# Top-k attention and ELU feed-forward on one core: in the first six steps, the mask begins where the selection ends, extra key transposes are spread, and raw weight tiles use other buffers

## The chip, the cores and the metric

One core of a Trainium2 chip runs the whole kernel. The metric is the device time of one execution, in microseconds (us); lower is better. Engines are named as in the profile: PE is TensorE (PEld its weight load), DVE is VectorE, ACT is ScalarE, POOL is GpSimd, SP is SyncE, which issues nearly all DMAs.

## What is computed

Attention over 8 batches, 8 heads, 576 tokens of 64 elements, in which each query keeps its 32 best keys, and then a two-layer network with ELU. The weights come as float64.

```python
scores = scale * np.matmul(q, k.transpose(0, 1, 3, 2))
kth = np.partition(scores, -top_k, axis=-1)[..., -top_k:-top_k + 1]
scores = np.where(scores >= kth, scores, -1000000000.0)
attn = np.exp(scores - np.max(scores, axis=-1, keepdims=True))
attn = attn / (np.sum(attn, axis=-1, keepdims=True) + 1e-09)
attn_out = np.matmul(attn, v)                      # (8, 8, 576, 64)
x = attn_out.transpose(0, 2, 1, 3).reshape(4608, 512)
h = x @ w_in                                       # (512, 2048)
g = np.where(h > 0.0, h, np.exp(np.minimum(h, 0.0)) - 1.0)
out = g @ w_out                                    # (2048, 512)
```

## The kernel before

**Steps.** The work is cut into 144 steps. A step is one tile of 128 query rows of a batch with one pair of heads (a pair of half tiles at the end of a batch). The order on every engine is the order in which the code is written: nothing is rescheduled, and each engine works through its own queue in order, waiting on semaphores where an input is not there. Step n of the loop (L676) holds the selection of tile n ("now"), the softmax and transposes of tile n-1 ("last"), and from step 6 on the attention product of tiles further back. A step does the following.

- `first_max` and `next_max` (L333 to L348), on DVE: eight largest of a row (MAX8, L336 and L348), strike them out (MATCH_REPLACE8, L342), four times over for two heads. This is the selection of the 32 best.
- the mask. From step 6 on `mask` (L357) does it on POOL with three operations for each half. For the tiles of steps 0 to 5 `mask_early` (L364) does it: a small `field` operation on DVE (L374), three small ones on POOL (L377, L378, L381: `minus`, `nth`, `pos`), then for each half an ACT activation (L386) and a POOL subtraction (L389), and at last `neg` (L355), which the exponential needs.
- `exp` (L398) on ACT, `trans` (L438, L456) on PE with copies on ACT (L443, L457): the transposed probabilities. `attend` (L471): the attention product on PE, and after the last pair of heads a copy to `xT` (L481).
- `sums` and `normalise`: the row sums' reciprocals are written to DRAM and read back as a broadcast (`recd`, `rb`, L413 and L425), and POOL multiplies `xT` by them (L486).
- `feed` puts pieces of the feed-forward network between: `hidden` (L506 on PE, L520 to L522 on ACT: `n`, `gT`, `n`; L523 on POOL) and `project` (L530). How many go into a step is worked out from counts alone when the program is built.

**Keys and queries.** `load_qk` loads a pair of heads from DRAM, `transpose_qk` turns it on PE (L268, L276; ten transposes into two PSUM tiles) and copies it to SBUF on ACT (L273, L281), and `keep_kq` stores it in DRAM, from where `load_kq` gets it again for later steps. The first four pairs belong to batch 0. Pairs 4 to 9 ("extra") are turned ahead of their need in steps 3, 4 and 5, and from step 7 on one pair in every second step (`turns`). The transposes, the scores (L311) and the probabilities share a pool of two PSUM tiles, so each of them waits until ACT has copied an earlier one out.

**Weights.** Each of 32 units of weights comes as raw float64 words and is turned into float32 in the first seven steps: `split_weight` on ACT (L185, L186, two activations), and two slots later `join_weight` on DVE (L191, L192) and POOL (the add of L196). `decode` places slots: four in each of steps 0 to 3 (places 3 to 6), six in steps 4 and 5, four in step 6. Slot i joins unit i-2 and splits unit i. So slots 18 to 23 lie in step 4, 24 to 29 in step 5 and 30 to 33 in step 6. Raw words lie in the pool "g", in spare buffers s1 to s4, or in rows of `w_out` that are not yet filled; the list `loads` (L144) says for each load its unit, its count, its home, and the unit that must have been joined first. In an early step the order after the start is:

```python
decode(n, 0); feed(n, 0.5); exp(last, 0); exp(last, 1)
next_max(now, (n, 1)); decode(n, 2); trans(last); feed(n, 0.5)
next_max(now, (n, 3)); decode(n, 4)
...                                   # sums(last), attend(last)
next_max(now, (n, 5)); decode(n, 6)
...                                   # normalise(last.g), extra transposes, loads
```

`mask_early(last)` stands at the very start of a step, ahead of the scores of a later step and after the last decode of the step before.

Of the kernel before, what the change touches and what calls it, by code (L numbers as in the profile page):

```python
# [11 lines left out]
U32 = mybir.dt.uint32  # L12
# [49 lines left out]
def kernel(  # L62
# [60 lines left out]
    WN = 512  # L123
    NW = 2 * NF
    raw = {}
    decoded = [0]

    def spare_tile(i, name):

        size = ((2 * J + 2) * P, 2 * S, 2 * WN)[i // 2]  # L130
        return spare.tile([P, size], FP32, tag=f"s{i}", name=name)
# [9 lines left out]

    loads = [(0, 3, "g", -1), (3, 1, "raw", -1), (4, 3, "g", -1), (7, 1, "raw", -1)]  # L144
    loads += [(8, 4, "w", -1), (12, 4, "w", -1), (16, 3, "g", 2), (25, 1, "raw", -1)]
    loads += [(26, 1, "raw", -1), (27, 1, "raw", 3), (19, 3, "g", 6)]
    loads += [(28, 1, "raw", 7), (22, 3, "w", 15), (29, 1, "raw", 25)]
    loads += [(30, 1, "raw", 26), (31, 1, "raw", 27)]
    places_in_w_out = {8: 0, 12: 8, 22: 10}

    turn = [0]

    def load_weights(most=NW, margin=1):

        while loads and most > 0 and (
            loads[0][3] < 0 or loads[0][3] + margin < decoded[0]
        ):
            i, n, home, _ = loads.pop(0)
            most -= 1
            if home == "w":  # L160
                at = places_in_w_out[i]
                t = w_out[:, at : at + 2 * n, :].bitcast(U32)
                t = t.rearrange("p (c f) d -> p c (f d)", f=2)
            elif home == "g":
                t = gpool.tile([P, n, 2 * WN], U32, tag="g", name="raw")[:]
            else:
                t = spare_tile(1 + turn[0] % 4, "raw")[:, 0 : 2 * WN].bitcast(U32)
                t = t.rearrange("p (c n) -> p c n", c=1)
                turn[0] += 1
            if i < NF:  # L170
                f, c = divmod(i, NC)
                src = moe_w_in[c * P : (c + n) * P, 2 * f * WN : 2 * (f + 1) * WN]
            else:
                src = moe_w_out[(i - NF) * P : (i - NF + n) * P, :]
            nc.sync.dma_start(t, src.rearrange("(c p) n -> p c n", p=P))
            for j in range(n):
                raw[i + j] = t[:, j, :]
# [38 lines left out]
    def load_qk(b, hp):  # L216

        first = b == 0 and hp < 3
        aside = (b, hp) in ((0, 1), (0, 2), (1, 1), (1, 2), (2, 0))
        if aside:  # L220
            home = xtpool.tile([P, 2, NC * T // 2], FP32, tag="xT", name="kqin")
            home = home[:, :, 0 : (J + 1) * 2 * D].rearrange(
                "p n (j h d) -> p n j h d", j=J + 1, h=2
            )
        for n, (name, src) in enumerate((("k", k), ("q", q))):
            queue = nc.scalar if first and name == "q" else nc.sync
            if aside:
                t = home[:, n]
            else:
                t = ldpool.tile([P, J + 1, 2, D], FP32, tag="in", name=name + "in")  # L230
            queue.dma_start(
                t[:, 0:J, :, :],
                src[b, 2 * hp : 2 * hp + 2, 0:JP, :].rearrange(
                    "h (p j) d -> p j h d", j=J
                ),
            )
            queue.dma_start(
                t[0:R, J, :, :],
                src[b, 2 * hp : 2 * hp + 2, JP:S, :].rearrange("h p d -> p h d"),
            )  # L240
            loaded[b, hp, name] = t
# [343 lines left out]
    EARLY = 6  # L585
    sizes = {0: (1, 1, 1, 1, 1, 1, 1, 2), 2: (2, 2, 2, 3), B - 2: (3, 3, 2, 1)}
    steps, first, order = [], {}, []
    for b in range(B):
# [4 lines left out]
        for qt in (0, 1, 2, 3, 4) if b % 2 == 0 else (4, 0, 1, 2, 3):  # L593
            r0 = b * S + (JP if qt == J else qt)
            if qt == J:
# [3 lines left out]
                c0, n = slot * P + (b % 2) * R, R  # L599
                rows = slice(r0, r0 + R)  # L600
            else:
                blk, slot = places.pop(0)
                c0, n = slot * P, P
# [20 lines left out]
    def decode(n, place):  # L624

        if place in ((1, 2, 3, 4, 5, 6) if n in (4, 5) else (3, 4, 5, 6)):
            weight_slot()
# [5 lines left out]

    pairs = [(b, hp) for b in range(B) for hp in range(NHP)]

    extra = {3: (4, 5, 6), 4: (7, 8), 5: (9,)}
    fetch = {2: (4, 5, 6), 3: (7, 8), 4: (9,), 5: (10,)}
    for p, pair in enumerate(pairs):
        if p >= NHP:
            n = next((n for n in extra if p in extra[n]), None)  # L640
            if n is None:
                n = EARLY + 1 + 2 * (p - 10)
                turns[n] = pair
            at(n + 1, keep_kq, *pair)
        elif p >= 2:
            at(p - 1, keep_kq, *pair)
# [11 lines left out]
    with tc.manual_schedule():  # L658
        for hp in range(3):
            load_qk(0, hp)  # L660
        load_weights(3)
        for hp in range(2):
            transpose_qk(0, hp)
            steps[hp].kq = {hp: kqT[0, hp]}
            for half in range(2):
                scores(steps[hp], half)
            if hp == 0:
                load_qk(0, 3)
        load_weights()
        load_v(0, 0)  # L670
        first_max(steps[0])
        weight_slot()
        weight_slot()
        for hp in range(2):
            keep_kq(0, hp)
        for n in range(NS + 4):  # L676
            early = n < EARLY
            now, last, done = (
                steps[n + d] if 0 <= n + d < NS else None for d in (0, -1, -2)
            )  # L680
            for fn, args in todo.pop(n, []):
                fn(*args)
            gone = None
            if early:
                if last:
                    mask_early(last)
                if n + 2 < NHP:
                    transpose_qk(0, n + 2)
                for m in direct.get(n, ()):
                    hp = m % NHP  # L690
                    steps[m].kq = {hp: kqT[0, hp]}
                    for half in range(2):
                        scores(steps[m], half)
            elif n % 2 == 0:

                for d in (2, 3):
                    if n + d < NS:
                        for half in range(2):
                            scores(steps[n + d], half)
                    if d == 2:  # L700
                        for u in steps[n - 4 : n - 2]:
                            if not u.attended:
                                attend(u)
                                gone = u
            if n in turns:
                transpose_qk(*turns[n])
            if n >= EARLY and n + 2 in turns:
                load_qk(*turns[n + 2])
            if now and n > 0:
                first_max(now)  # L710
            if last and not early:
                biases(last, early)
                mask(last, 0)
            if early:
                decode(n, 0)
                feed(n, 0.5)
                if last:
                    exp(last, 0)
                    exp(last, 1)
                next_max(now, (n, 1))  # L720
                decode(n, 2)
                if last:
                    trans(last)
                feed(n, 0.5)
                next_max(now, (n, 3))
                decode(n, 4)
                if last and last.ends:
                    load_weights(margin=0)
                    sums(last)
                if last:  # L730
                    attend(last)
                next_max(now, (n, 5))
                decode(n, 6)
                if last and last.ends:
                    normalise(last.g)
                for p in extra.get(n, []):
                    transpose_qk(*pairs[p])
                for p in fetch.get(n, []):
                    load_qk(*pairs[p])
                continue  # L740
            decode(n, 0)
            feed(n, (0.3, 0.7)[n % 2])
            if now:
                next_max(now, (n, 1))
            decode(n, 2)
            if last:
                mask(last, 1)
                exp(last, 0)
            if done and not done.turned:
                trans(done)  # L750
            if now:
                next_max(now, (n, 3))
            decode(n, 4)
            if gone and gone.ends:
                normalise(gone.g)
            feed(n, (0.3, 0.7)[n % 2])
            if now:
                next_max(now, (n, 5))
            decode(n, 6)
            if last:  # L760
                exp(last, 1)
            if done and done.ends and not done.summed:
                sums(done)
        while ffn:
            ffn.pop(0)[1]()
# [33 lines left out]
```

## Time and profile before

| | |
|---|---|
| time, median of 3 (lowest to highest) | 1663.04 us (1661.5 to 1663.15) |
| the profiled execution | 1664.04 us, of which its span is 1662.3 |
| busy: PE, DVE, POOL, ACT | 1571.1, 1455.5, 1142.7, 925.7 us |
| the chain that ended last, by engine | PE 60%, DVE 24%, POOL 5%, issue 4%, ACT 4% |
| DVE busy in 0 to 20, 20 to 40, 40 to 60 us | 8.06, 17.46, 19.32 |
| mean granted PE clock | 0.974 |

The span runs from the first to the last instruction. Busy time is summed by engine; the chain is followed back from the last instruction, from each to what released it. A list in order of time shows for each instruction its start, its length, its line, its tiles, and in brackets how long the engine was idle ahead of it and what ended that. The table of stretches gives for each stretch the busy time of PE, PEld, DVE, ACT and POOL, the granted PE clock as a share of full speed, and the share and the rate of the transfers. Line numbers are those of the kernel before; behind L144 the changed kernel's are smaller by 3, as its list is shorter.

### The profile page before, as it was taken

How to read it: one execution, taken by the hardware profiler on the slowest of the kernel's cores; microseconds unless marked ns; L12 is line 12 of the kernel's file. 1: busy time of each engine (PE TensorE's matmuls, PEld its weight loads, DVE VectorE, ACT ScalarE, POOL GpSimd, SP SyncE). 2: the span in 40 equal slices, each digit the busy share in tenths (PEclk: the TensorE clock that was granted, in tenths of full speed). 3: DMA queues.
4: the chain of work that ended last, by engine and by line, in shares of the span. 5: the costliest groups of instructions: out<-in, count | busy, mean ns of one | idle time of the engine just before them, and what ended most of it. 6: DMA issues, size and time to landing. Idle time of an engine off the chain costs nothing.

```text
span 1662.3 us, 28290 instructions
## 1 busy us (share of the span) xinstructions
PE 1571.1 (95%) x9792; PEld 1046.9 (63%) x9792; DVE 1455.5 (88%) x3070; ACT 925.7 (56%) x1887; POOL 1142.7 (69%) x1457
## 2 busy tenths in 40 slices
PE   5559999999999999999999999999999999999999
PEld 3346777777776775757566566566556566566565
DVE  6889999999999999999999989979989989987000
ACT  6666665656665564646465476466456466355121
POOL 3567777777777786878778678668668668668021
PEclk7579999999999999999999999999999999999999
DMA  9853555444453513121212321221222312210000
GB/s 316 243 192 117 166 182 154 151 127 142 143 169 93 190 46 110 65 84 70 85 70 100 112 88 61 77 85 64 91 70 100 112 59 90 77 42 8 26 7 13
DMA packets 138895, 174.49 MB, mean 105 GB/s; under 512 B 94208, under 2 KB 102400, under 8 KB 138752
## 3 DMA queue, kind: packets, MB, share of 16 engines
q1 hardware_dynamic: 135200, 171.80, 32.3%
q8 instruction: 78, 1.28, 0.3%
q10 hardware_dynamic: 3552, 0.89, 0.3%
q14 instruction: 65, 0.53, 0.1%
HBM read 144.18 MB, written 28.46 MB: 104 GB/s over the span
## 4 chain that ended last, share of the span: by engine, by line
PE 60%; DVE 24%; POOL 5%; issue 4%; ACT 4%; DMA 2%; SPq 1%; ACTq 0%; POOLq 0%; DVEq 0%
PE ops L530 21%; PE hps L506 19%; DVE m L348 11%; DVE wk L342 10%; PE scps L311 7%; PE avps L471 6%; PE eps L438 5%; DVE m L336 2%; POOL sc L362 1%; POOL gT L523 1%; PE qkps L268 1%; ACT sc L398 1%; POOL wk L360 1%; POOL wk L361 1%; DMA rb<-recd 1%
## 5 line engine op out<-in xcount | busy, mean ns | idle before, releaser
L348 DVE MAX8 m<-wk 128x8 f32<-128x576 f32 x864 | 609.5, 747 | 0.0
L506 PE MATMUL hps<-xT,w_in 128*128 128x128 f32 (+2 forms) x2432 | 531.4, 373 | 10.4 <-ACT gT L521 5.8
L530 PE MATMUL ops<-w_out,gT 128*128 128x512 f32 x1152 | 519.6, 596 | 7.6 <-ACT osb L539 7.6
L506 PEld LDWEIGHTS hps<-xT,w_in 128*128 128x128 f32 x2432 | 381.1, 192 | 134.8 <-issue 17.7
L342 DVE MATCH_REPLACE8 wk<-m,wk 128x576 f32<-128x576 f32 x576 | 423.4, 743 | 0.0
L362 POOL TENSOR_TENSOR sc<-sc,wk 128x576 f32<-128x576 f32 x278 | 392.6, 1412 | 23.3
L398 ACT ACTIVATE sc<-sc,neg 128x576 f32<-128x576 f32 x288 | 224.0, 778 | 251.0 <-POOL sc L362 245.1
L530 PEld LDWEIGHTS ops<-w_out,gT 128*128 128x128 f32 x1152 | 209.6, 190 | 240.9 <-issue 213.8
L523 POOL TENSOR_TENSOR gT<-gT,n 128x384 f32<-128x384 f32 (+1 forms) x168 | 187.6, 1124 | 178.2 <-ACT n L522 174.2
L360 POOL TENSOR_SCALAR wk<-sc,nth 128x576 f32<-128x576 f32 x278 | 208.0, 748 | 27.0
L311 PE MATMUL scps<-kq 64*128 64x288 f32 (+3 forms) x1344 | 187.1, 428 | 31.2 <-ACT kq L273 20.7
L342 DVE MATCH_REPLACE8 wk<-m,sc 128x576 f32<-128x576 f32 x288 | 211.7, 743 | 0.0
L336 DVE MAX8 m<-sc 128x8 f32<-128x576 f32 x288 | 201.2, 740 | 11.3 <-ACT sc L331 11.1
L331 ACT COPY sc<-scps 128x576 f32<-128x576 f32 x288 | 170.0, 639 | 73.8 <-PE scps L311 71.9
L361 POOL TENSOR_SCALAR wk<-wk 128x576 f32<-128x576 f32 x278 | 185.7, 668 | 23.0
L443 ACT COPY et<-eps 128x1024 f32<-128x1024 f32 x144 | 144.5, 1003 | 90.6 <-PE eps L438 89.7
L471 PE MATMUL avps<-et,vE 128*64 128x128 f32 (+1 forms) x3200 | 179.6, 268 | 5.3 <-ACT et L443 5.3
L471 PEld LDWEIGHTS avps<-et,vE 128*64 128x64 f32 x3200 | 161.7, 139 | 32.3 <-issue 24.8
L438 PEld LDWEIGHTS eps<-ident,sc 128*128 128x128 f32 x1152 | 135.3, 142 | 72.3 <-issue 36.6
L438 PE MATMUL eps<-ident,sc 128*128 128x128 f32 x1152 | 153.2, 276 | 21.8 <-ACT sc L398 19.6
L311 PEld LDWEIGHTS scps<-kq 64*128 64x128 f32 (+1 forms) x1344 | 104.6, 180 | 103.1 <-issue 31.3
L520 ACT ACTIVATE n<-hps 128x384 f32<-128x384 f32 (+1 forms) x168 | 90.3, 537 | 108.8 <-PE hps L506 102.8
(66 smaller groups left out, 927.6 us busy)
## 6 DMA issues: line engine op xcount, KB each, us to landing
kq<-kqd SPq DMA_DIRECT2D x152, 576.0 KB
kqd<-kq SPq DMA_DIRECT2D x32, 576.0 KB
rb<-recd SPq DMA_DIRECT2D x64, 128.0 KB
out_dram<-osb SPq DMA_DIRECT2D x32, 256.0 KB
kin<-in_k_dram SPq DMA_DIRECT2D x27, 256.0 KB
qin<-in_q_dram SPq DMA_DIRECT2D x26, 256.0 KB
w_out<-in_moe_w_in_dram SPq DMA_DIRECT2D x2, 2048.0 KB
vE<-in_v_dram SPq DMA_DIRECT2D x32, 128.0 KB
```

Source lines behind the costliest of these rows:

```text
L311: nc.tensor.matmul(ps[rows, j, at : at + keys.stop - keys.start], u.kq[hp][r, 1, q0 : q0 + g.ql], u.kq[hp][r, 0, keys], start=True, stop=True,
L336: nc.vector.max(u.m1[:, i, :], u.sc[:, i, :])
L342: nc.vector.match_replace(u.wk[:, i, :], u.m[:, i, :], u.cur[:, i, :], TAKEN)
L348: nc.vector.max(u.m[:, i, :], u.cur[:, i, :])
L360: nc.gpsimd.tensor_scalar(pen, s, u.nth[:, i : i + 1], 2.0**100, ALU.add, ALU.mult)
L362: nc.gpsimd.tensor_tensor(s, s, pen, ALU.add)
L398: nc.scalar.activation(s, s, AF.Exp, bias=u.neg[:, i : i + 1], scale=scale, accum_out=g.den[:, at : at + 1],)
L438: nc.tensor.transpose(ps[:, i, c * P : (c + 1) * P], e[:, k0 + c * P : k0 + (c + 1) * P], ident[:],)
L471: nc.tensor.matmul(g.av[r, hp, 0:ql], vE[g.b, hp][:, i, (c + i) % (J + 1), :], u.et[:, at, q0 : q0 + ql], start=(c == 0), stop=(c == J),)
L506: nc.tensor.matmul(ps[:, f % G, :], w_in[:, i, f * P : (f + 1) * P], blk.xT[:, i, 0:N], start=(i == 0), stop=(i == NC - 1),)
L523: nc.gpsimd.tensor_tensor(g, g, n, ALU.subtract)
L530: nc.tensor.matmul(blk.o[:], blk.gT[f // NG][:, f % NG, s * P : (s + 1) * P], w_out[:, f, :], start=(f == 0), stop=(f == NF - 1),)
```

## The change

Three things, all about the first six steps.

- `mask_early` is called for the step's own tile, behind its last `next_max` and ahead of the last decode, instead of at the start of the next step. So the tile of step 5 gets the early mask as well, and step 6 has no mask of its own.
- One extra pair in each of steps 3, 4 and 5 is turned in mid step, right behind `trans(last)`; steps 3 and 4 turn a second one at their end. Pair 9 is no longer an extra one: it is turned in step 7, and every later pair two steps later than before, the last in step 51. Pair 8 is loaded to the usual buffers, not to one of `xT`'s.
- The raw tiles of units 22 to 31 are loaded in another order and to other homes.

```diff
-    loads = [(0, 3, "g", -1), (3, 1, "raw", -1), (4, 3, "g", -1), (7, 1, "raw", -1)]
-    loads += [(8, 4, "w", -1), (12, 4, "w", -1), (16, 3, "g", 2), (25, 1, "raw", -1)]
-    loads += [(26, 1, "raw", -1), (27, 1, "raw", 3), (19, 3, "g", 6)]
-    loads += [(28, 1, "raw", 7), (22, 3, "w", 15), (29, 1, "raw", 25)]
-    loads += [(30, 1, "raw", 26), (31, 1, "raw", 27)]
-    places_in_w_out = {8: 0, 12: 8, 22: 10}
+    loads = [(0, 3, "g", -1), (3, 1, 1, -1), (4, 3, "g", -1), (7, 1, 2, -1)]
+    loads += [(8, 4, "w", -1), (12, 4, "w", -1), (16, 3, "g", 2), (26, 1, 3, -1)]
+    loads += [(22, 1, 1, 3), (19, 3, "g", 6), (24, 1, 2, 7), (28, 1, 4, -1)]
+    loads += [(23, 1, "w", 13), (25, 1, "w", 14), (27, 1, "w", 15)]
+    loads += [(29, 1, 1, 22), (30, 1, 2, 24), (31, 1, 3, 26)]
+    places_in_w_out = {8: 0, 12: 8, 23: 10, 25: 12, 27: 14}
...
-                t = spare_tile(1 + turn[0] % 4, "raw")[:, 0 : 2 * WN].bitcast(U32)
+                t = spare_tile(home, "raw")[:, 0 : 2 * WN].bitcast(U32)
...
-        aside = (b, hp) in ((0, 1), (0, 2), (1, 1), (1, 2), (2, 0))
+        aside = (b, hp) in ((0, 1), (0, 2), (1, 1), (1, 2))
...
-    extra = {3: (4, 5, 6), 4: (7, 8), 5: (9,)}
-    fetch = {2: (4, 5, 6), 3: (7, 8), 4: (9,), 5: (10,)}
+    extra = {3: (4, 5), 4: (6, 7), 5: (8,)}
+    fetch = {2: (4, 5, 6), 3: (7,), 4: (8,), 5: (9,)}
...
-                n = EARLY + 1 + 2 * (p - 10)
+                n = EARLY + 1 + 2 * (p - 9)
...
             if early:
-                if last:
-                    mask_early(last)
                 if n + 2 < NHP:
...
-            if last and not early:
+            if last and n > EARLY:
                 biases(last, early)
                 mask(last, 0)
...
                 if last:
                     trans(last)
+                for p in extra.get(n, [])[:1]:
+                    transpose_qk(*pairs[p])
                 feed(n, 0.5)
...
                 next_max(now, (n, 5))
+                mask_early(now)
                 decode(n, 6)
                 if last and last.ends:
                     normalise(last.g)
-                for p in extra.get(n, []):
+                for p in extra.get(n, [])[1:]:
                     transpose_qk(*pairs[p])
...
             if last:
-                mask(last, 1)
+                if n > EARLY:
+                    mask(last, 1)
                 exp(last, 0)
```

More of the change, by code (lines that the diff above doesn't have):

```diff
@@ L137, in weight @@
         return w_out[:, i - NF, :]
-    loads = [(0, 3, "g", -1), (3, 1, "raw", -1), (4, 3, "g", -1), (7, 1, "raw", -1)]
-    loads += [(8, 4, "w", -1), (12, 4, "w", -1), (16, 3, "g", 2), (25, 1, "raw", -1)]
-    loads += [(26, 1, "raw", -1), (27, 1, "raw", 3), (19, 3, "g", 6)]
-    loads += [(28, 1, "raw", 7), (22, 3, "w", 15), (29, 1, "raw", 25)]
-    loads += [(30, 1, "raw", 26), (31, 1, "raw", 27)]
-    places_in_w_out = {8: 0, 12: 8, 22: 10}
-    turn = [0]
+    loads = [(0, 3, "g", -1), (3, 1, 1, -1), (4, 3, "g", -1), (7, 1, 2, -1)]
[4 more added lines that the diff above has]
+    places_in_w_out = {8: 0, 12: 8, 23: 10, 25: 12, 27: 14}
     def load_weights(most=NW, margin=1):
@@ L166, in load_weights @@
             else:
-                t = spare_tile(1 + turn[0] % 4, "raw")[:, 0 : 2 * WN].bitcast(U32)
+                t = spare_tile(home, "raw")[:, 0 : 2 * WN].bitcast(U32)
                 t = t.rearrange("p (c n) -> p c n", c=1)
-                turn[0] += 1
             if i < NF:
```

## The prediction

> **What bounds the kernel now.** I read the page first, then the table of stretches, then the time-ordered lists of VectorE (DVE), ScalarE (ACT), GpSimd (POOL) and TensorE (PE) up to 150 us. The table of stretches gives busy us of PE, PEld, DVE, ACT and POOL, then the granted clock:
>
> ```profile
> 60.00:80.00 20.00, 11.70 (x59) 9.37 (x59) 19.31 (x40) 13.04 (x23) 9.75 (x13) 0.52 0.69 155
> 80.00:100.00 20.00, 12.81 (x68) 9.01 (x69) 12.49 (x29) 16.61 (x31) 12.64 (x12) 0.67 0.72 236
> 100.00:120.00 20.00, 11.00 (x82) 9.80 (x80) 17.67 (x29) 11.98 (x22) 14.05 (x16) 0.76 0.43 145
> 120.00:140.00 20.00, 17.84 (x123) 14.34 (x123) 20.00 (x38) 12.96 (x25) 16.68 (x17) 0.86 0.89 275
> ...
> 400.00:800.00 400.00, 388.26 (x2618) 279.54 (x2615) 399.25 (x850) 237.16 (x474) 306.22 (x392) 1.00 0.34 109
> 800.00:1200.00 400.00, 396.14 (x2257) 237.86 (x2256) 381.83 (x805) 222.77 (x477) 296.73 (x387) 1.00 0.25 85
> ```
>
> From 118 to 800 us DVE never rests; from 800 PE fills 396 of 400. The order on both is unchanged there, so whatever DVE gains or loses by step 7 moves everything behind it by the same amount. Before 118 DVE has holes, and its list names them (start, us, line; the idle time ahead and its releaser in brackets):
>
> ```profile
> 39.09 0.43 DVE L191 TENSOR_SCALAR w_in<-w_in 128x512 uint32<-128x512 uint32 x1 [1.83 <-ACT w_in L185]
> ...
> 87.60 0.43 DVE L191 TENSOR_SCALAR w_out<-w_out 128x512 uint32<-128x512 uint32 x1 [7.31 <-ACT w_out L185]
> ...
> 107.28 0.54 DVE L191 TENSOR_SCALAR w_out<-w_out 128x512 uint32<-128x512 uint32 x1 [2.27 <-ACT w_out L185]
> ...
> 112.20 0.95 DVE L191 TENSOR_SCALAR w_out<-w_out 128x512 uint32<-128x512 uint32 x1
> 113.07 1.78 DVE L192 SCALAR_TENSOR_TENSOR raw<-raw 128x512 uint32<-128x512 uint32 x1
> ```
>
> With 0.43, 0.54 and 0.55 more at 22.75, 54.17 and 69.27, the holes are 12.9 us. Each is a join waiting for its split, and ACT is late with the split. The last two lines show another loss: joins stretched (0.33 and 0.60 is the undisturbed step from one to the next) while a POOL add holds them up; these come to 0.74 in each of steps 1 to 3 and to about 6.8 us from 101 to 135. Steps begin (first MAX8 of L336) at 26.25, 42.62, 57.69, 72.79, 96.29, 118.04 and 134.42 for steps 1 to 7.
>
> **The change, part by part.** I write split i and join i for weight unit i; slot i does join i-2, then split i.
>
> *Mask at the end of its own step.* Today L374 follows the last join, POOL then does that join's add and two memsets, and ACT's L386 starts 2.68 us after the next step began (45.30 against 42.62). Moved ahead of the join, L374 comes 0.93 earlier and POOL is free of the add: start of L377 to start of L386 took 0.94 undisturbed (28.00 to 28.94) and 1.41 beside a join (99.16 to 100.57). I take 1.41, so L386 starts 0.5 after the next step and exp, behind 2.78 of POOL subtraction and neg, at 4.6 instead of 6.8: 2.2 earlier. Step 1: exp is held by pair 3's copies and scores instead, now at 29.55 instead of 30.48, so the hole at 39.09 shrinks by 0.93. Step 2: split 10 is ready before DVE asks; the hole of 0.54 is gone and the stretched join (0.74) costs about 0.36, as POOL's delayed add of slot 9 lies there. Steps 2 and 3 then begin at 41.7 and 55.85, 0.9 and 1.85 earlier. Step 5's mask moves from POOL's three operations a half (0.75 + 0.67 + 1.41) to the early form: POOL saves some 2.9 us in step 6.
>
> *Pair 4's transposes in mid step 3.* exp at 60.5, probabilities' copy 2.98 later (49.42 to 52.40) at 63.45; PSUM frees at 64.45; eight transposes at the half clock take 1.97, pair 4's copy starts at 66.45, split 14 follows 1.07 later at 67.5 and is ready at 68.2. DVE asks at 66.35. So here the change makes a hole of 1.9 where 0.55 was. Queued behind the copy on ACT are splits 14 to 16 and the next mask; on PE the attention product. Step 4 begins at 71.75, 1.0 earlier. Pair 4's data must be there at 64.45: the loads up to it are 19.8 MB, and the rates of the stretches (5.48 + 7.14 + 6.54 MB by 60 us, then 250 and 214 GB/s) put it at 62.7.
>
> *One pair instead of three at the end of step 3.* Today three chained copies (73.06, 76.15, 79.22) and the mask stand ahead of exp at 85.37. Now: mask 72.3, split 17 73.8, pair 5's copy 74.95, then as today 6.15 from the last copy to exp (79.22 to 85.37): 81.1. Split 18 is ready at 83.2; DVE joins at 83.25 instead of 87.60, hole 2.9 instead of 7.3. Next: the probabilities' copy at 84.8, pair 6's transposes 85.8 to 87.8, its copy, split 20 ready at 89.7; DVE asks at 88.7, a new hole of 1.0. Step 5 begins at 93.2, 3.1 earlier.
>
> *Step 5, where it is given back.* POOL's and PE's lists of today:
>
> ```profile
> 97.92 1.27 POOL L486 TENSOR_TENSOR xT<-xT,rb 128x512 f32<-128x512 f32 x1 [0.24 <-issue]
> 99.16 0.40 POOL L377 TENSOR_SCALAR minus<-field 128x2 f32<-128x2 uint32 x1
> ...
> 104.79 0.22 POOL L355 TENSOR_SCALAR neg<-m 128x2 f32<-128x2 f32 x1
> ```
> ```profile
> 99.25 5.49 PE L506 MATMUL hps<-xT,w_in 128*128 128x128 f32 x24 [1.36 <-POOL xT L486]
> 105.97 1.41 PE L438 MATMUL eps<-ident,sc 128*128 128x128 f32 x8 [1.23 <-ACT sc L398]
> ```
>
> Today xT goes ahead of the mask, and PE does its 24 hidden matmuls while the mask and exp run. In the new order POOL does mask (L386 93.75, subtractions to 97.9, neg 98.3), the add of join 21 (99.6), then xT to 101.0. exp is done at 99.8, but PE stands at hps, which starts at 101.05 instead of 99.25, so the transposes of the probabilities come at 106.4, no earlier than today's 105.97. Behind them now stand pair 8's transposes (1.1 at the full clock) and copy, then n, gT, n (1.55) and only then split 26: at 112.6, ready 113.3. Today split 26 starts at 111.40. DVE asks at 108.2 (12.0 undisturbed from the step's start, and 3.0 of stretches beside the mask and the adds, which the hole covers in any case): a new hole of 5.2 in place of the 2.27 at 107.28. POOL's gT waits for n too, with the adds of joins 24 to 26 and the mask of step 5 queued behind it; they then run back to back beside slots 28 and 29 and stretch these by 0.7, 1.2 and 0.75 (rows 112.20 to 116.10 show 0.54, 1.1, 1.0). Step 6 begins at 119.1, 1.0 later than today.
>
> [...]
>
> *Step 6.* The mask is done (POOL: subtractions 120.45 to 123.25), exp at 125.7, splits 30 and 31 in time. Undisturbed the step is 9.66 + 4 x 0.93 = 13.4; adds and gT cost about 1.4 more, today 2.9 to 3. Step 7 begins at 133.8, against 134.42: 0.6 earlier.
>
> *Raw tiles.* Unit 29 is now asked for after the add of 22, not 25; ACT's 4.60 wait for it at 114.9 goes, but DVE showed no hole there, so nothing is won directly. New: unit 28's split writes the row in which raw unit 25 lies and waits for its add at 116.75; it is needed at 124.9, so the cover is 7 us. SP meets recd, rb and pair 8's load in the old order; pair 8 should land near 98, needed at 108.5. Free.
>
> *One transpose pair moves from step 5 to step 51.* PE 1.4 us and ACT 1.3 at the full clock. Bounds 0 and 1.4; the stretches from 540 to 620, which have such pairs in every second step, show DVE at 19.93 to 20.00, so 0. No gain either: it is the same work.
>
> Sum, by the lengths of steps 1 to 6: today 16.4, 15.1, 15.1, 23.5, 21.75 and 16.4, in the walk 15.4, 14.2, 15.9, 21.45, 25.9 and 14.7, so -0.9, -0.9, +0.8, -2.05, +4.15, -1.7: net -0.6. The profiled execution took 1664.04 (span 1662.3 and 1.7 around it), 1.0 over the median of 1663.04; off the median: 1662.4.
>
> **Rivals.** *Faster: the clock.* PE's gaps shrink in steps 4 and 5. At the full clock 16 score matmuls (4.51 at the half) save 2.2, pair 6's transposes 0.9, the 24 matmuls up to 2.4: split 26 then comes near 107 to 108, the hole at slot 28 closes, and 5.2 + 0.6 is kept: 1657.2. Against: 0.50 in nearly all of 62 to 84 although PE was 12 of 20 busy. For: 1.00 from 105 to 115.
>
> *Slower: pair 4 comes late.* Two raw tiles (1.05 MB), not one, now stand directly ahead of it on SP. It has 1.75 us in hand; past 64.45 each us delays split 14, and through it every step of the chain to split 26, one for one. From 65.0 the change loses; past 68.4 by over 0.2%. Lower bound 62.7, upper 69, when the burst of three pairs ends (transfer share 0.17 from 70): then 4.5 - 0.6 = +3.9: 1667.
>
> *It doesn't reach the end.* Were PE's own work the limit already from 120, step 7's 0.6 would be lost: 1663.0. Against it, DVE at 399.25 of 400; it lies inside no change.
>
> **Chances.** A measurement of this kernel can tell about 0.2%, 3.3 us, from no change. The walk, and not reaching the end, 0.52, between 1659.8 and 1666; the clock 0.30; pair 4 late or a like delay in the chain 0.18. Range 1657 to 1667, which leaves out the far half of both rivals.
>
> **What would show it.** Right: DVE's first holes gone or under 1 us, about 2 at slot 16, 3 at slot 20, and one of about 5 near 113 that ends on ACT's L182 (the new number of L185); xT after neg, near 100; eps of step 4 behind hps; step 7 at 133 to 135. Wrong: no hole at slot 28, or hps at the full clock; pair 4's transposes waiting for a DMA; DVE idle after 120.

## The result, and the profile after

The changed kernel takes 1663.75 us (median of 12, 1662.89 to 1667.29), the kernel before, beside it, 1662.38 (median of 12, 1660.21 to 1664.09): ratio 1.0011, 95% interval 1.0002 to 1.0020. It is slower by a tenth of a per cent, where 0.04% faster was forecast. The time lies in the range given, the sign is wrong. The profiled execution took 1663.52 (span 1661.7).

DVE's holes in the changed kernel, as they were shown for the kernel before (start, us, line; idle time ahead of it and releaser):

```profile
38.09 0.43 DVE L188 TENSOR_SCALAR w_in<-w_in 128x512 uint32<-128x512 uint32 x1 [1.44 <-ACT w_in L182]
...
67.78 0.43 DVE L188 TENSOR_SCALAR w_in<-w_in 128x512 uint32<-128x512 uint32 x1 [1.96 <-ACT w_in L182]
...
82.85 0.43 DVE L188 TENSOR_SCALAR w_out<-w_out 128x512 uint32<-128x512 uint32 x1 [1.60 <-ACT w_out L182]
...
89.22 0.43 DVE L188 TENSOR_SCALAR w_out<-w_out 128x512 uint32<-128x512 uint32 x1 [0.86 <-ACT w_out L182]
...
112.18 1.03 DVE L188 TENSOR_SCALAR w_out<-w_out 128x512 uint32<-128x512 uint32 x1 [3.95 <-ACT w_out L182]
```

These are the five holes of the forecast's walk, which had 0.9 in step 1, 1.9 in the middle of step 3, 2.9 and 1.0 in step 4, and 5.2 near 113 in step 5. The order on GpSimd and TensorE in step 5 is the one foreseen too, xT behind `neg`, the hidden matmuls behind xT, the transposes of the probabilities behind those (first GpSimd's list, then TensorE's):

```profile
97.32 0.65 POOL L352 TENSOR_SCALAR neg<-m 128x2 f32<-128x2 f32 x1
97.95 1.28 POOL L193 TENSOR_TENSOR w_out<-w_out,raw 128x512 uint32<-128x512 uint32 x1
99.19 1.50 POOL L483 TENSOR_TENSOR xT<-xT,rb 128x512 f32<-128x512 f32 x1
```
```profile
100.74 4.71 PE L503 MATMUL hps<-xT,w_in 128*128 128x128 f32 x24 [8.97 <-POOL xT L483]
105.29 1.04 PE L435 MATMUL eps<-ident,sc 128*128 128x128 f32 x8
```

The table of stretches (busy PE, PEld, DVE, ACT, POOL, then the granted clock) shows where DVE's work went:

```profile
60.00:80.00 20.00, 13.31 (x65) 9.56 (x65) 17.86 (x34) 13.05 (x23) 13.28 (x16) 0.59 0.94 248
80.00:100.00 20.00, 7.80 (x51) 6.21 (x49) 17.15 (x35) 16.31 (x31) 11.99 (x13) 0.67 0.44 139
100.00:120.00 20.00, 11.89 (x91) 10.57 (x91) 16.02 (x26) 10.63 (x19) 10.94 (x12) 0.84 0.38 127
120.00:140.00 20.00, 17.84 (x115) 15.26 (x115) 20.00 (x39) 13.32 (x26) 15.10 (x16) 0.79 0.81 237
...
400.00:800.00 400.00, 389.52 (x2623) 280.10 (x2621) 399.24 (x849) 237.50 (x475) 306.07 (x391) 1.00 0.36 112
```

From 80 to 100 us DVE is busy 17.15 where it was 12.49, from 60 to 80 and from 100 to 120 some 1.5 less each; behind 120 nothing differs. Lengths of steps 1 to 6, from one first MAX8 to the next:

| | 1 | 2 | 3 | 4 | 5 | 6 | sum |
|---|---|---|---|---|---|---|---|
| before, the profile the forecast used | 16.37 | 15.07 | 15.10 | 23.50 | 21.75 | 16.38 | 108.17 |
| forecast for the changed kernel | 15.4 | 14.2 | 15.9 | 21.45 | 25.9 | 14.7 | 107.55 |
| changed, profiled | 15.47 | 13.71 | 15.99 | 21.45 | 25.31 | 15.43 | 107.36 |

So the walk of the new order held within 0.75 us in every step and 0.2 in the sum; that the sum is nearer than the steps is luck, as steps 2 and 5 came 0.5 and 0.6 shorter and step 6 0.7 longer. The error of the forecast must be looked for in what this was subtracted from.

### The profile page after: what moved, and what is told of

Read it like the earlier page. It is cut to its first block, busy times and chain, and to the rows that moved or that the text cites. A ratio compares the mean times of both kernels' runs of the same rounds, so it can differ in the third digit from the quotient of the medians.

```text
span 1661.7 us, 28294 instructions
## 1 busy us (share of the span) xinstructions
PE 1569.8 (94%) x9792; PEld 1046.7 (63%) x9792; DVE 1456.9 (88%) x3071; ACT 926.7 (56%) x1889; POOL 1141.3 (69%) x1456
## 4 chain that ended last, share of the span: by engine, by line
PE 64%; DVE 21%; ACT 4%; POOL 4%; issue 4%; DMA 2%; SPq 1%; ACTq 0%; POOLq 0%
PE ops L527 22%; PE hps L503 21%; DVE m L345 10%; DVE wk L339 9%; PE scps L308 7%; PE avps L468 7%; PE eps L435 5%; DVE m L333 2%; POOL sc L359 1%; PE qkps L265 1%; DMA kq<-kqd 1%; POOL gT L520 1%; ACT sc L395 1%; POOL wk L357 1%; POOL wk L358 1%
## 5 line engine op out<-in xcount | busy, mean ns | idle before, releaser
L517 ACT ACTIVATE n<-hps 128x384 f32<-128x384 f32 (+1 forms) x168 | 90.2, 537 | 112.6 <-PE hps L503 104.2
```

## The experiments

Two theories. The first: the walk is right, but the profile of before was one of its long executions, so the gain of 0.6 was taken from a number that the median doesn't have. The second: the change sets off a loss that the profile of the first six steps doesn't show.

### Both kernels again

No edit: copies of the two kernels, timed again, and a third profile of each.

> The kernel before, unchanged, for a second profile and a time against itself. Theory 'clock phase': the first profile of before had the 24 hidden matmuls of step 5 at the half clock throughout (5.49 us), which is the worst case, so another profile shows step 7 beginning up to 1.5 us earlier (132.9 to 134.4) and the stretch from step 7 to the end at 1527.9 within 0.5. Rival 'later stage': step 7 begins at 134.4 within 0.3 again. Rival 'spread only': ratio to itself differs from 1 by as much as 0.1%.

> The changed kernel, unchanged, for a second profile. 'Clock phase': the first profile of it had the hidden matmuls at 4.71 us; with them at 5.49, step 6 begins near 119 and step 7 at 134.3 to 135.5, and from step 7 to the end it takes 1528 as in before; ratio 1.0005 to 1.0015. 'Later stage': step 7 at 133.6 within 0.3, and 1 to 2 us more than 1528 from there to the end. 'Spread only': ratio 0.9995 to 1.0005.

> The kernel before, a third profile. In the first, steps 1 to 6 took 108.2 us from the start of step 1 to that of step 7, in the second 107.45, the difference lying in step 4 (hole of 7.31 against 5.98) beside a start-up 1.0 shorter. Theory 'clock phase': it lies within 106.5 and 108.3, and the hole of step 4 is nearer to 6 than to 7.3; start of step 1 anywhere from 25.2 to 27.2. Rival 'same early part in every execution': 108.2 again.

> The changed kernel, a third profile. Steps 1 to 6 took 107.4 and 106.5 us in the first two, in executions that were at the lower end of its times (hidden matmuls 4.71 and 4.30). Theory 'clock phase': with the matmuls at 5.2 to 5.5 it takes 107.5 to 108.5; from step 7 to the end 1528 to 1529 as in all others. Rival 'later stage': 106.5 to 107.4 again, and over 1529 from step 7 to the end.

before_again took 1662.91, ratio 1.0000 (0.9991 to 1.0009); after_again 1665.11, ratio 1.0010 (1.0001 to 1.0019): the small loss is there twice. Single times of the third profiles: 1662.73 and 1663.12. The profiles:

| | steps 1 to 6 | of it step 4 | hole of step 4 | step 7 to the end | that execution |
|---|---|---|---|---|---|
| before, three profiles | 108.17, 107.45, 104.72 | 23.50, 22.18, 21.31 | 7.31, 5.98, 5.11 | 1527.88, 1528.48, 1529.18 | 1664.04, 1662.97, 1662.73 |
| changed, three profiles | 107.36, 106.54, 106.73 | 21.45, 21.24, 21.37 | 1.60, 1.41, 1.54 | 1528.09, 1528.35, 1528.08 | 1663.52, 1663.18, 1663.12 |

The first six steps of before vary by 3.45 us between executions, those of the changed kernel by 0.82. The forecast stood on the longest of three. The means are 106.78 and 106.88: the six steps gain nothing that three profiles could show, as a mean of three that lie so far apart is uncertain by about 1 us (an estimate from their spread). The third profile of before also lies under the 106.5 to 108.3 expected of it. Step 1 itself, which the table leaves out, begins at 26.25, 25.27 and 27.00 in the kernel before and at 26.25, 26.51 and 26.49 in the changed one. Why step 4 varies is seen on TensorE at the end of step 3 of the kernel before, in the first and in the third profile (start, us, what, idle time ahead):

```profile
74.14 1.97 PE L268 MATMUL qkps<-ident,kqin 128*128 128x128 f32 x8 [0.82 <-ACT kq L273]
...
77.21 1.97 PE L268 MATMUL qkps<-ident,kqin 128*128 128x128 f32 x8 [0.70 <-ACT kq L273]
...
80.28 4.51 PE L311 MATMUL scps<-kq 64*128 64x288 f32 x16 [0.70 <-ACT kq L273]
```
```profile
74.88 1.09 PE L268 MATMUL qkps<-ident,kqin 128*128 128x128 f32 x8 [1.58 <-ACT kq L273]
...
77.07 1.09 PE L268 MATMUL qkps<-ident,kqin 128*128 128x128 f32 x8 [0.84 <-ACT kq L273]
...
79.27 3.93 PE L311 MATMUL scps<-kq 64*128 64x288 f32 x16 [0.84 <-ACT kq L273]
```

The same eight transposes take 1.97 in one and 1.09 in the other, and the granted clock from 70 to 84 us is 0.50 and 0.80. From the attention product (68.55 and 69.28) to the exponential it is 16.82 and 14.61, and the hole is 7.31 and 5.11: the difference of 2.2 passes through one for one. before_again lies between, clock 0.71, 15.50, hole 5.98. So the kernel before wins 1.3 and 2.2 us in this chain where the clock of these 14 us is 0.71 and 0.80 instead of 0.50; the changed kernel, with two of the three pairs gone from it, varies by 0.21 us in step 4. Most of the rest, 1.38 us, lies in step 6 (16.38, 16.61 and 15.00): the last join's second half, beside an add on GpSimd, takes 1.78 in the first profile and 0.68 in the third.

### One part alone

mask_only is the kernel before with `mask_early(now)` ahead of the last decode and nothing else. transposes_only and raw_only are the kernel before with the other two parts, mask_undone the changed kernel with the mask put back:

```diff
-                mask_early(now)
                 decode(n, 6)
...
+                if last:
+                    mask_early(last)
                 if n + 2 < NHP:
```

> The kernel before with the mask moved to the end of its step, and nothing else of the change. The walk: steps 2, 3 and 4 begin at 41.7, 55.4 and 69.4 (no transposes in mid step 3), then three chained pairs hold exp until about 84.9 and the join of slot 20 until 87.1, pairs 7 and 8 and xT behind the mask hold split 26 until 113; step 7 at 134.5 to 135.5; ratio 1.0000 to 1.0012. If moving the mask is by itself the gain of 2.2 us in each step that its own chain shows: step 7 near 130, ratio 0.997.

> The kernel before with only the spreading of the extra key transposes: one pair in the middle of each of steps 3, 4 and 5, a second at the end of steps 3 and 4, pair 9 in step 7; the mask stays at the start of the next step and the raw tiles stay as before. Theory (the walk, step by step): the late exp of step 3 (some 2.2 us later than in the changed kernel) makes the hole at slot 16 about 4 instead of 1.96, so step 4 begins near 75.9; one pair instead of three at the end of step 3 shortens the hole of slot 20 to about 2, step 5 begins near 94.6, pair 8 in mid step 5 gives a hole of 4 to 5 at slot 28, step 7 near 134.2; ratio to before 0.9995 to 1.0005. Rival (the spreading is what wins and the mask is what costs): step 7 two or more us earlier than in the kernel before, at 130 to 131, ratio 0.9985 or less.

> The kernel before with only the new order and homes of the raw weight tiles. Theory (the walk): DVE showed no hole at the wait that goes, so nothing moves: step lengths as in the kernel before, step 7 at 131.7 to 134.4 like its three executions, ratio 1.0000 within 0.0008. Rival (two raw tiles stand ahead of pair 4's loads, and the key loads come late): the three chained copies at the end of step 3 start later, step 4 above 24 us, ratio 1.001 or more.

> The changed kernel with the mask put back to the start of the next step (step 5's as three operations a half): the kernel before plus the spread transposes plus the raw tiles' new homes. Theory (the spreading puts pair 4 in the middle of step 3, which only an early exponential can bear, so the loss of the spreading alone is the late mask): a hole of 3.6 at slot 16 as with the transposes alone, step 4 begins near 76.5, step 7 near 138 to 139, ratio to before 1.004 to 1.006. Rival (raw tiles and transposes belong together, the raw tiles clear the way for the key loads): ratio 1.002 or less.

| kernel | median (n) | ratio to before, interval | steps 1 to 6 of its profile |
|---|---|---|---|
| mask_only | 1664.38 (11) | 1.0006 (0.9997 to 1.0015) | 107.17 |
| transposes_only | 1669.92 (5) | 1.0048 (1.0034 to 1.0062) | 111.74 |
| raw_only | 1665.94 (9) | 1.0019 (1.0009 to 1.0029) | 108.03 |
| mask_undone | 1670.48 (5) | 1.0044 (1.0031 to 1.0058) | 111.64 |

No part is a gain by itself. The mask alone brings step 4 forward by 3.65 us (42.89 behind step 1, not 46.54). Step 4 then takes 26.38: the second halves of its first two joins are stretched (1.89 and 1.78, where the kernel before has 0.68), and DVE waits for the three copies longer than before:

```profile
86.43 0.43 DVE L191 TENSOR_SCALAR w_out<-w_out 128x512 uint32<-128x512 uint32 x1 [7.71 <-ACT w_out L185]
113.00 1.05 DVE L191 TENSOR_SCALAR w_out<-w_out 128x512 uint32<-128x512 uint32 x1 [2.37 <-ACT w_out L185]
```

The transposes alone lose 7 us, far outside the ratio expected. Step 3 was as worked out (18.16, step 4 begins 49.61 behind step 1), but the exponential in step 5 is late too, and there the hole at slot 28 adds to that of slot 26:

```profile
73.41 0.43 DVE L191 TENSOR_SCALAR w_in<-w_in 128x512 uint32<-128x512 uint32 x1 [3.62 <-ACT w_in L185]
...
107.79 0.52 DVE L191 TENSOR_SCALAR w_out<-w_out 128x512 uint32<-128x512 uint32 x1 [3.64 <-ACT w_out L185]
117.00 1.06 DVE L191 TENSOR_SCALAR w_out<-w_out 128x512 uint32<-128x512 uint32 x1 [4.24 <-ACT w_out L185]
```

mask_undone is as slow as transposes_only, 1.0044 where the changed kernel was at 1.0010 and 1.0011: the early mask is what makes the spread transposes bearable, as the theory said, and the raw tiles belong to neither. Alone the raw tiles cost 0.19% where I had said nothing; its first six steps are as long as before's longest (step 4 is 23.50), and in its profile the loss lies behind step 7 (1532.95 to the end, against 1527.9 to 1529.2). That execution, 1669.82, is the slowest of its nine. Some 4 us of the loss stand in steps 12, 13, 80 and 81, behind the stretches at half clock told of below (here the first is at 0.50 from 171 to 177 us); why it should meet more of them was not found.

### Where a pair is turned

pair4_end and pair8_end are the changed kernel with pair 4 at the end of step 3, or pair 8 at the end of step 5. The diff is pair 8's; for pair 4 it has `n > 3`:

```diff
-                for p in extra.get(n, [])[:1]:
+                for p in extra.get(n, [])[: n < 5]:
...
-                for p in extra.get(n, [])[1:]:
+                for p in extra.get(n, [])[n < 5 :]:
```

> The changed kernel with pair 4 turned at the end of step 3, ahead of pair 5, instead of in the middle of it; pairs 6 and 8 stay in the middle of steps 4 and 5. Theory (each pair's copy delays what stands behind it on ScalarE, wherever it is put): the hole of 1.96 at slot 16 is gone and step 3 is 13.7 to 14.0 long instead of 16.0, but two chained copies then stand ahead of step 4's exponential, some 3 us later, so the hole of slot 20 grows from 1.6 to about 4.7 or 5: step 4 near 24.5, step 5 begins where it did or 1 us later, ratio to before 1.001 to 1.0015. Rival (the middle of a step is the bad place for any pair, as it was for pair 8): step 5 begins 1.5 us or more earlier than 93, ratio to before 1.0000 or less.

> The changed kernel with pair 8 turned at the end of step 5 instead of its middle. If pair 8's transposes and copy are a link of the chain to split 26: split 26 starts 2.3 earlier (near 109.1), step 6 begins about 2 earlier, the copy (1.15) comes back in step 6 ahead of the scores' copies, where a slack of about 1.5 takes it; time 1.5 to 2 us below the changed kernel, ratio to before about 0.9995. If the copy is hidden in the wait for the hidden matmuls anyway: no difference to the changed kernel, 1.001.

pair4_end: 1664.65 (11), ratio 1.0016 (1.0008 to 1.0025). Slot 16 has no hole any more, step 3 is 13.71, and step 4 pays for it; the forecast's arithmetic again:

```profile
83.22 0.43 DVE L188 TENSOR_SCALAR w_out<-w_out 128x512 uint32<-128x512 uint32 x1 [4.67 <-ACT w_out L182]
```

pair8_end: 1661.00 (11), ratio 0.9989 (0.9980 to 0.9997), faster than both kernels, and by more than the 1.5 to 2 us expected against the changed one. The hole at slot 28 falls from 3.95 to 2.05:

```profile
111.24 1.03 DVE L188 TENSOR_SCALAR w_out<-w_out 128x512 uint32<-128x512 uint32 x1 [2.05 <-ACT w_out L182]
```

Steps 5 and 6 take 23.42 and 14.12 instead of 25.31 and 15.43. By time pair4_end can't be told from the changed kernel; its first six steps are 107.86, 1.0 us over that kernel's mean. So pair 4 stands no worse in mid step, and pair 8 does: at the end of step 5 no copy stands ahead of an exponential that DVE will wait for.

### The clock and the order in step 5

xt_first puts `normalise` ahead of `mask_early(now)`, so that xT precedes the mask on GpSimd. after_warm puts five unused matmuls at the end of step 4, meant to have the clock at 1.00 when the hidden matmuls come (a profile shows each of the five as two records):

```diff
+                if last and last.ends:
+                    normalise(last.g)
                 mask_early(now)
                 decode(n, 6)
-                if last and last.ends:
-                    normalise(last.g)
```
```diff
+                if n == 4:
+                    warm = ps_o.tile([P, dm], FP32, tag="o", name="warm")
+                    for _ in range(5):
+                        nc.tensor.matmul(
+                            warm[:], ident[:], w_in[:, 0, 0:WN], start=True, stop=True
+                        )
```

> The changed kernel with xT's normalisation put ahead of the mask of step 4 on GpSimd, all else as in the change. If the give-back is the chain xT, hidden matmuls, transposes of the probabilities, pair 8's copy, split 26: the hidden matmuls start near 94.5, exp of step 4 comes 2 later, split 26 starts near 108.6 instead of 111.45, the hole at slot 28 shrinks by 2 to 3 us, and the time falls by about 2.7 us against the changed kernel, ratio to before about 0.9990. If that chain is not what holds slot 28, the later mask costs up to 2 us: ratio 1.002.

> The changed kernel with five extra matmuls (identity by a decoded weight tile, into the still unused PSUM tile of the projection) on TensorE at the end of step 4, where it waits 9 us for xT; their result is used by nothing. They are to hold the granted clock at 1.00 until the hidden matmuls. If the hidden matmuls' half clock is a link of the chain to split 26: these take 2.8 to 3.3 instead of 4.3 to 5.5, slot 28's hole shrinks by 1.2 to 2, ratio to before 0.9995 to 1.0003 where the changed kernel has 1.0010. If the clock there doesn't matter: ratio 1.0010.

xt_first: 1663.64 (11), ratio 1.0006 (0.9998 to 1.0015), not the 0.9990 expected. The hidden matmuls start at 94.64 as foreseen and the transposes of the probabilities at 101.55, nearly 4 us earlier than in the changed kernel. But the exponential is later by the time of xT, a hole of 2.26 opens at slot 26, and 3.25 is left at slot 28: step 5 is as long as the changed kernel's. The lead is lost before split 26, which starts at 111.33 as against 111.45: two splits keep the probabilities' copy until 104.39, and the 20 hidden matmuls, for the first of which n waits, take 3.89 where the changed kernel has 2.50:

```profile
107.73 3.89 PE L503 MATMUL hps<-xT,w_in 128*128 128x128 f32 x20
```

after_warm: 1664.95 (11), ratio 1.0010 (1.0001 to 1.0019), no gain. Behind the unused matmuls TensorE pauses for 4.90 us, and the hidden matmuls then take 5.49, where the changed kernel's first profile has 4.71:

```profile
91.40 4.56 PE L742 MATMUL warm<-w_in,ident 128*128 128x512 f32 x10
100.85 5.49 PE L503 MATMUL hps<-xT,w_in 128*128 128x128 f32 x24 [4.90 <-POOL xT L483]
```

So these took 0.23 us each, as in the first profile of before, where the 20 that come later in the changed kernel take 0.125; what shorter ones would be worth there was not tested. feed_late takes the 24 matmuls out of the chain. It is pair8_end with the feed-forward pieces of a step moved behind the fourth weight slot:

```diff
                 decode(n, 0)
-                feed(n, 0.5)
                 if last:
                     exp(last, 0)
...
-                feed(n, 0.5)
                 next_max(now, (n, 3))
                 decode(n, 4)
+                feed(n, 0.5)
+                feed(n, 0.5)
```

> The kernel with pair 8 turned at the end of step 5, and in addition the two pieces of feed-forward work of an early step moved behind the step's fourth weight slot: on TensorE the transposes of the probabilities stand ahead of the 24 plus 20 hidden matmuls, on ScalarE splits 26 and 27 stand ahead of n, gT, n, on GpSimd the two adds stand ahead of gT. Theory (the hole at slot 28 is the chain xT, hidden matmuls, transposes, copy, ELU, split): the transposes follow the exponential at once, near 100.6 instead of 106.8, split 26 starts near 104.2 instead of 110.5, the hole of 2.05 at slot 28 is gone, step 5 is about 21.4 instead of 23.4, step 7 begins near 129.4 instead of 131.4, and the time is about 1659.0, ratio to before 0.9977. Rival (the end does not follow step 7, as TensorE's own work, which now starts later, is the bound from there): step 7 comes early as above, but the time stays at 1661, ratio 0.9989; or DVE is held in step 6 by the later gT and adds, step 6 above 15.5, and the same ratio.

1657.18 us (median of 5, 1657.00 to 1657.63), ratio 0.9967 (0.9955 to 0.9980): the best of the study, and more than expected. TensorE's list, then ScalarE's:

```profile
98.91 1.97 PE L435 MATMUL eps<-ident,sc 128*128 128x128 f32 x8 [6.87 <-ACT sc L395]
...
100.89 7.06 PE L503 MATMUL hps<-xT,w_in 128*128 128x128 f32 x44
```
```profile
101.77 1.00 ACT L440 COPY et<-eps 128x1024 f32<-128x1024 f32 x1
...
103.66 0.68 ACT L182 ACTIVATE w_out<-raw 128x512 f32<-128x512 f32 x1 [0.73 <-POOL w_out L193]
```

The transposes start 0.9 behind the exponential's start (7.9 in pair8_end), though they take 1.97 where pair8_end has 1.04; split 26 stands right behind their copy, at 103.66 where pair8_end had 110.50. The hole at slot 28 is gone, and its joins, 1.03 and 1.78 long in pair8_end beside GpSimd's adds, take 0.42 and 0.69, as the adds no longer queue behind gT. The expectation had counted the hole alone: step 5 takes 19.58, not 21.4, and steps 1 to 6 take 100.37. That is 6.4 less than the mean of before, and 5.7 arrive in the time; from step 7 to the end its profile has 1529.25, 0.7 over the mean of before's three.

### Behind step 7

The executions also differ by jumps behind step 7. In the third profile of before there is one of 0.87 + 0.66 us at steps 80 and 81. TensorE ahead of it, in the first profile of before and then in the third:

```profile
773.46 1.30 PE L311 MATMUL scps<-kq 64*128 64x288 f32 x8 [1.61 <-ACT sc L331]
774.68 2.86 PE L506 MATMUL hps<-xT,w_in 128*128 128x256 f32 x12
```
```profile
770.45 1.29 PE L311 MATMUL scps<-kq 64*128 64x288 f32 x8 [1.62 <-ACT sc L331]
771.67 4.54 PE L506 MATMUL hps<-xT,w_in 128*128 128x256 f32 x12
```

The same twelve instructions, behind the same pauses of 1.7 and 1.6 us, take 2.86 or 4.54; in the third profile the granted clock is 0.50 for about 3.4 us (772.0 to 775.4). The 1.7 lost stay hidden while DVE is the limit, and 1.5 of them appear eight steps later, where TensorE becomes it. Such stretches, some of them 6.8 us long, stand near 147, 175, 633 or 775 us in eight of the fifteen profiles without a fill, and in none of the changed kernel's three; ahead of them TensorE's lists show pauses (3.03 us in transposes_only near 145, 4.62 in raw_only near 171, 2.30 near 628 in the third profile of before). Beside the first profile of before, all five profiles with the stretch near 775 are longer by 1.5 us in steps 80 and 81, and no other is; all five with one between 170 and 182 are longer by 0.65 to 2.5 us in steps 12 and 13, and no other is. Those near 147 and 633 leave 0.3 us at most in the steps that follow. before_fill, after_fill and feed_late_fill put eight unused matmuls into those pauses:

```diff
+    def warm(k, space=None):
+        t = (space or ps_h).tile([P, WN], FP32, tag="o" if space else "h", name="warm")
+        for _ in range(k):
+            nc.tensor.matmul(t[:], ident[:], w_in[:, 0, 0:WN], start=True, stop=True)
...
+            if f == part == 0 and step[0] == 10:
+                warm(2)
...
+                if step[0] in (57, 58):
+                    warm(2)
...
+                    if n in (8, 72):
+                        warm(1, ps_o if n == 72 else None)
```

> The kernel before with eight unused 128x512 matmuls (0.91 us each) put into five pauses of TensorE behind the first six steps: one ahead of each of two score groups of step 8, two ahead of the hidden matmuls that wait for xT in step 10, two ahead of the project group that waits for its PSUM tile in step 58, one ahead of each of two score groups of step 72. Their results are used by nothing. Theory (what differs between executions behind step 7 is a stretch of 3.4 us at half clock that follows such pauses): no stretch below clock 1.00 between 140 and 1600 us is left, the time from step 7 to the end is 1528 or less, the median is 0.5 to 1.5 us lower, 1661.2 to 1662.2, and the range of the times shrinks from 5 us to about 3 (what is left is the first six steps). Rival (the clock drops elsewhere, or TensorE's own pauses are not what counts): the same median as before, 1662.5 to 1663, and the same range.

> The changed kernel with the same eight unused matmuls in the same five pauses. Theory (its upper half of times, near 1665.5, has a stretch at half clock behind step 7): the upper half goes, the median is near 1663, 1 to 2 us under the changed kernel's, and within 1 us of before_fill's. Rival (the difference lies in the first six steps): the same distance of 1 to 2 us to before_fill as between the two kernels without the fill.

> The kernel feed_late with the same eight unused matmuls. Its five times lay between 1657.0 and 1657.6 and its profile has no stretch of half clock behind step 7. Theory: there is nothing to win, 1657 within 0.7; some of the pauses are shorter here, so up to 0.5 us may be lost. Rival (fewer pauses make PE's own work end earlier in any case): 1656 or less.

No stretch at half clock is left between 140 us and 1600 in any of the three profiles: each of the stretches of 20 us has 1.00. before_fill: 1662.41 (11, 1660.58 to 1663.67), ratio 0.9996 (0.9988 to 1.0005), lower and with a smaller range as expected, though the interval does not leave out an equal time; after_fill: 1663.53 (11, 1661.34 to 1665.28), ratio 1.0002 (0.9993 to 1.0011); the kernel before took 1663.42 (1660.02 to 1664.85) beside them. feed_late_fill: 1657.05 (5), ratio 0.9964 (0.9951 to 0.9976), nothing won over feed_late, as it should. Of the changed kernel's first twelve times three were above 1665, of its eleven second times six; of after_fill's eleven, one is. That points to stretches behind step 7 as the cause of the upper part of its times, but the counts are small. And 1.1 us between the two filled kernels remain, as the rival of after_fill had it, though the intervals overlap: that the whole of the difference lies behind step 7 is not shown.

## Why the prediction missed, point by point

- **What bounds the kernel, and that a gain by step 7 reaches the end.** Right: pair8_end and feed_late, in steps 1 to 6 shorter by 2.7 and 6.5 us than the changed kernel's mean, beat its two medians by 2.8 to 4.1 and by 6.6 to 7.9 us.
- **The mask.** Right in what it frees (steps 1 and 2 at 15.47 and 13.71, forecast 15.4 and 14.2), in step 1 with some luck: its hole shrinks by 0.39, not 0.93, and the rest comes from a join that takes 0.48 where the kernel before has 1.15. It also carries the transposes: without it they cost 0.44% to 0.48%.
- **Pair 4 in mid step 3, one pair instead of three.** Right in its steps: holes of 1.96, 1.60 and 0.86 against 1.9, 2.9 and 1.0. The smaller second hole comes with joins stretched ahead of it (1.89 and 1.77), which the walk did not have there; step 4 is 21.45 in both, as the split that ends this hole came when foreseen (DVE joins 11.4 us behind the step's start, forecast 11.5).
- **Step 5, where it is given back.** Right in its chain: hidden matmuls at 100.74 (forecast 101.05), split 26 at 111.45 (112.6), hole 3.95 (5.2). The matmuls took 4.71, not the 5.49 of the row of before that the walk used; after_warm and xt_first show 5.49 again, so both occur, by execution. The changed kernel's other two profiles have 4.30 and 4.37.
- **The sum: here it failed.** "Sum, by the lengths of steps 1 to 6: today 16.4, 15.1, 15.1, 23.5, 21.75 and 16.4 ... net -0.6", then taken off the median. The 23.5 of step 4 is the half-clock case of the kernel before (0.50 from 70 to 84 us); three profiles have 23.50, 22.18 and 21.31, and its six steps 104.7 to 108.2, mean 106.78. Against that mean the walk's own 107.55 is a loss of 0.8, not a gain of 0.6, and the changed kernel's mean of 106.88 is a loss of 0.1. I then took off 1.0, by which the profiled time lay over the median, as if the changed kernel had this excess too; but its profiled 1663.52 lies 0.2 under its median. Without that step the forecast is 1663.4, and 1663.75 came: the time was foreseen and the gain was not there.
- **The clock as a rival.** I let it shorten only the changed kernel. That smaller gaps would bring the full clock to steps 4 and 5 was an assumption: in the stretches from 80 to 100 and 100 to 120 us the changed kernel has 0.67 and 0.84, the kernel before 0.67 and 0.76. The clock shortens the kernel before more: there three pairs of transposes and sixteen score matmuls chain on TensorE and ScalarE, and step 4 differs by up to 2.2 us; the changed kernel's differs by 0.21.
- **Pair 4 late, and not reaching the end.** Neither happened: pair 4's transposes waited 0.94 for ScalarE's copy, not for a load, and step 7's differences arrive.
- **Raw tiles, "Free".** Beside the transposes no cost shows (mask_undone 1.0044, transposes_only 1.0048); alone 0.19%, cause open.

What stays open: where the 0.1% itself lies. Three profiled executions of each kernel take the same time on average (1663.25 and 1663.27); the slower half of the changed kernel's times was never profiled. Two close relatives of it were: after_warm at 1667.47 and pair4_end at 1666.19. Their first six steps are 107.44 and 107.86, and from step 7 to the end they take 3.4 and 2.5 us more than the changed kernel's mean, 2.3 us of it in steps 12, 13, 80 and 81. Whether the changed kernel meets such stretches more often than the kernel before, or whether the raw tiles' new homes cost it something, is not shown: no kernel with the other two parts alone was run.

## What to carry to other kernels

When a forecast is a difference of two walks, both must be typical executions: take two or three profiles of the kernel before and compare step by step before believing a gain smaller than their spread. Work that is moved to other steps (here the key transposes) takes its wait along, to wherever its copy stands ahead of something that the bounding engine will ask for; ask for each place what is queued behind it. When an engine's slow work delays a chain, moving it behind the chain (feed_late, -0.33%) did what feeding it earlier (xt_first) did not; the attempt to speed it up (after_warm) did not reach it.

## What the runs showed of the hardware

Identical code differs by execution, and with it the granted TensorE clock: eight transposes of the kernel before take 1.97 us in the first profile, where the clock from 72 to 76 us is 0.50, and 1.09 in the third, where it is 0.97; 24 hidden matmuls take 4.28 (raw_only) to 5.49 (the first profile of before, xt_first, after_warm). One stretch of some 3.4 us at 0.50, in the third profile of before, costs 1.7 us of TensorE time (4.54 against 2.86 for the same twelve matmuls), behind pauses of 1.7 and 1.6 us that cost nothing in the first profile. TensorE was busy for 1.55 of the 3 us ahead of it (769 to 772 us). Why such a stretch comes in one execution and not in another is not shown.
